# A new order of all operations in an attention-then-feed-forward kernel, with one store moved ahead of the next loads

## The chip, the cores and the metric

The kernel runs on one core of a Trainium2 chip. A core has five engines that run side by side, each through its own queue in order: TensorE (PE; its weight loads are listed as PEld), VectorE (DVE), ScalarE (ACT), GpSimd (POOL) and SyncE (SP). The last two, here, mainly issue DMAs. The metric is device microseconds of one execution, as a median over runs. A profile is one further execution with every instruction recorded.

## What is computed

Linear attention with cosine and sine weights, then a feed-forward block with a squared ReLU. There are 8 batches of 8 heads, 576 positions and 64 channels; the block works on 4608 tokens of 512 values with a hidden width of 2048.

```python
def phi(x, c, s):
    r = np.maximum(x, 0.0)
    return np.concatenate([r * c, r * s], axis=-1)
q_p = phi(q, cos_w, sin_w)
k_p = phi(k, cos_w, sin_w)
kv = np.einsum('bhsf,bhsd->bhfd', k_p, v)
z = np.sum(k_p, axis=2)
num = np.einsum('bhsf,bhfd->bhsd', q_p, kv)
den = np.einsum('bhsf,bhf->bhs', q_p, z)[..., None] + 1e-06
x = (num / den)  # heads beside each other: 4608 x 512
h = x @ w_in
r = np.maximum(h, 0.0)
g = r * r
out = g @ w_out
```

## The kernel before

Each batch goes through two parts. In the attention part, keys, queries and values are loaded (`ldk`, `ldq`, `ldv`: `load_main` at L513, `load_v` at L526), turned into features by eight wide operations (`cos` and `sin`, `feature` at L448), values are cast into a shared tile (`vs`, `spread_v` at L536), the matrix kv is summed on TensorE (`kv`, `mm_kv`) and copied out (`kvz`). Query features are transposed by DMA (`qTd`, L670), multiplied with kv (`num`), divided on VectorE (`div`: an add, a reciprocal and a product) and transposed by DMA again (`xTd`, L679). One load tile `kq` holds keys and queries of a batch, and from batch 2 on a feature operation handles both at once, so it needs both loads. The last 64 of the 576 positions are tails; two batches share a tile for them (`ldkt`, `ldqt`, and the operations with `t` or `.4` in their names).

In the feed-forward part both matrix products are done, from a point in batch 2 on, with seven block products in place of eight (Strassen-Winograd): `G{batch}.{quarter}.P1` to `P7` for the first (`plan_gemm1`, L960), `Y{batch}.P1` to `P7` for the second (`plan_pair`, L1159). `xs`, `S` and `w1s`, `w2t` are the sums of blocks that go in, made on VectorE. Results stand in PSUM banks and are taken out by ScalarE or VectorE: `seed`, `u2`, `s5` are copies, `c11r` and the like apply the ReLU and `c11q` the square. For `Y`, `c11`, `c12`, `c21`, `c22` write the four blocks of a batch's two output tiles `y`, and `st0` and `st1` store those two (512 KB each, `store` at L1089, issued by SP at L1097). There are two `y` tiles, so a batch's second tile is the one that the batch before stored with its `st1`: `Y2.c22` can only write when `Y1.st1` has landed. There are six PSUM banks for all products (`pool("x", 6)`) and one double bank for kv sums and numerators (`pool("n", 1)`): a product that needs a bank waits for the operation that empties it. For example `G3.3.P5` takes the bank that `Y2.c12` empties, and `num4.3` the one that `div4.1` empties.

What runs when is written out by hand, as a table of names: `ORDER` (L24 to L113). `Plan.run` (L220) takes it word by word; a `*` puts an operation on ScalarE that could be on either ScalarE or VectorE. The operations are issued in that order, so each engine's queue is the table's words for that engine, in the table's order. SP's queue holds loads, DMA transposes and stores, and a word there that must wait holds all that stand behind it. The same function assigns PSUM banks and tiles, from costs that stand beside each operation. A part before the table (`begin`, L1361) starts batch 0, and `loads_of_1` (L1490) issues batch 1's loads and weights on POOL's queue.

Four lines of the table before, round the place that matters:

```python
G3.0.P3 vs4.1* G3.0.c11r* G3.1.P1 Y2.P6 G3.0.u2* xs3.3 G3.0.P7 ldk5 div3.4 xs3.4 cos4.tk* kv4
ldv5.0 G3.1.seed G3.1.P2 ldq5 Y2.S3 Y2.u2* Y2.c11* Y1.st1 kvz4* G3.1.P6 num4.0 vs5.2 G3.0.c22r
...
G3.1.c21r* Y2.s5* G3.2.c11r* num4.1 div4.1 xTd3.2 vs5.0 sin5.3 G3.2.P6 G3.2.u2* Y2.P7 Y2.c22
sin5.0 ldv5.1 xTd4.0 Y2.P3 Y2.c12 Y2.st0 num4.3 div4.3 xTd4.1 cos5.1* cos5.3* G3.2.P5 G3.3.P1
```

Of the kernel before, what the change touches and what calls it, by code (L numbers as in the profile page):

```python
# [35 lines left out]
w2t3 xTc1.2 num1.3 vs2.0 ldv2.1 xT1.0 div1.3 Y0.c01* Y0.b12 Y0.b13 Y0.b14 ldkt2 Y0.b15 Y0.c11
ldqt2 xTc1.0* H1.3.00.0 Y0.c10 H1.3.00r* xT1.3 xTc1.3* cos2.1 sin2.0 cos2.2 cos2.0* sin2.1*
H1.2.00.0 H1.2.00r* sin2.2* cos2.3 sin2.3 Y0.st1 H1.0.01.0 H1.1.11.0 H1.1.11r* cos2.tk vs2.1*
H1.0.11.0 H1.0.11r* sin2.tk H1.1.00.0 H1.1.00r H1.3.00q H1.2.10.0 H1.1.11q* qTd2.0 H1.2.10r
qTd2.1 H1.2.01.0 ldk3 ldv3.0 H1.1.10.0 H1.1.10r* H1.3.10.0 kv2 kvz2* H1.0.10.0 num2.1 ldv3.2  # L40
H1.2.01r* ldq3 H1.0.00.0 w2t2 w2t4 H1.3.10r* H1.3.10q* div2.1 H1.1.01.0 H1.0.00r H1.1.01r num2.2
div2.2 H1.2.11.0 H1.0.01r* H1.1.01q H1.1.00q* H1.0.10r* H1.1.10q H1.3.11.0 H1.3.01.0 H1.2.11r*
H1.3.11r* H1.3.11q Y0.st0 num2.3 H1.3.01r* H1.3.01q Y1.P10 Y1.P11 div2.3 xTd2.1 Y1.seed Y1.P20
Y1.seed1 num2.0 vs3.0* Y1.S1 Y1.P21 vs3.2* Y1.P5 ldv3.1 Y1.S2 Y1.P6 ldv4.2 H2.1.10.0 cos3.1*
H2.0.11.0 div2.0 xTd2.0 sin3.1 cos3.0 sin3.0* qTd3.0 sin3.3* Y1.S3 Y1.u2 Y1.P7 cos3.3* H2.1.10r*
H2.0.11r* H2.0.00.0 Y1.c111* H2.1.00.0 sin3.2 cos3.2 qTd3.1 xs2.3 Y1.c110 xs2.1 xs2.2 vs3.1*
H2.0.00r ldq4 kv3 Y1.S4 xs2.4 H2.1.00r* vs4.2* G2.2.P1 kvz3 ldv4.0 sin3.tq H2.0.01.0 H2.0.01r
ldk4 num3.0 H2.1.11.0 div3.0 Y1.s5* Y1.c22 cos3.tq* G2.2.seed H2.1.11r* H2.1.11q H2.0.10.0
H2.1.00q* num3.1 div3.1 H2.0.10r* H2.1.01.0 w1s3 H2.1.01r* H2.1.01q* Y1.P3 H2.1.10q* num3.2
Y1.c12 div3.2 G2.2.P2 G2.2.c11r* vs4.0* G2.2.P6 ldkt4 G2.2.u2 G2.2.P5 G2.3.P1 G2.3.seed ldv5.2  # L50
ldkt5 num3.3 qTd3.2 xTd3.0 div3.3 G2.2.s5* G2.3.P5 G2.3.s5* G2.2.P7 G2.2.c22r G2.3.P2 G2.3.c11r*
G2.3.P6 xTd3.1 G2.3.u2 G2.2.P3 G2.2.P4 ldv4.1 cos4.1* G2.3.c11q G2.3.P3 sin4.1* Y1.st0 G2.3.P7
cos4.0 G2.3.c22r Y2.P1 cos4.3 sin4.0 G2.2.c21r* G2.2.c12r qTd4.0 cos4.2* G2.3.P4 G2.3.c21r
sin4.3* Y2.seed num3.4 Y1.P4 sin4.2 qTd4.1 G2.3.c21q* xs3.1 G3.0.P1 G3.0.P5 Y2.P2 G2.3.c12r
G2.3.c12q G2.3.c22q* G3.0.seed G3.0.P2 xs3.2 G3.0.P6 Y1.c21* Y2.S1 Y2.S2 sin4.tk G3.0.s5*
G3.0.P3 vs4.1* G3.0.c11r* G3.1.P1 Y2.P6 G3.0.u2* xs3.3 G3.0.P7 ldk5 div3.4 xs3.4 cos4.tk* kv4
ldv5.0 G3.1.seed G3.1.P2 ldq5 Y2.S3 Y2.u2* Y2.c11* Y1.st1 kvz4* G3.1.P6 num4.0 vs5.2 G3.0.c22r
G3.0.P4 ldqt1 G3.0.c12r div4.0 G3.1.c11r* G3.1.u2* G3.0.c21r* G3.1.P5 G3.1.s5* G3.1.P7 G3.1.c22r
G3.2.P1 G3.2.seed Y2.S4 num4.2 div4.2 G3.1.P3 Y2.P5 G3.1.c12r G3.1.P4 G3.2.P2 G3.1.c11q*
G3.1.c21r* Y2.s5* G3.2.c11r* num4.1 div4.1 xTd3.2 vs5.0 sin5.3 G3.2.P6 G3.2.u2* Y2.P7 Y2.c22  # L60
sin5.0 ldv5.1 xTd4.0 Y2.P3 Y2.c12 Y2.st0 num4.3 div4.3 xTd4.1 cos5.1* cos5.3* G3.2.P5 G3.3.P1
G3.3.P5 cos5.2 G3.2.s5* G3.2.P3 G3.2.P7 G3.2.c22r G3.2.c12r G3.3.seed G3.3.P2 G3.3.P6 G3.3.s5*
G3.3.P3 G3.2.P4 G3.3.u2* G3.3.c11r* sin5.2* G3.2.c21r* cos5.0 ldqt0 sin5.1 qTd5.0 G3.3.P7
G3.3.c22r Y2.P4 G3.3.c11q qTd5.1 G3.1.c21q* vs5.1* ldv6.2 ldv6.0 G3.3.P4 G3.3.c22q* Y3.P1
G3.3.c12r G3.3.c12q G3.3.c21r ldk6 Y3.seed xs4.1 G4.0.P1 G4.0.P5 G3.1.c12q* G4.0.seed G4.0.s5*
G3.3.c21q xs4.2 G3.1.c22q Y3.S1 Y3.S2 xs4.4 kv5 Y3.P2 kvz5* num5.0 Y3.S4 Y2.c21* G4.0.P6
G4.0.u2* xs4.3 sin1.tq* G4.0.P2 G4.0.c11r* G4.1.P1 G4.0.P3 div5.0 G4.0.c12r Y3.c11* Y3.P6 ldq6
G4.1.seed num5.2 div5.2 G4.0.P7 G4.0.c22r cos1.tq* Y3.u2* G4.1.P2 G4.1.c11r* G4.1.P6 G4.1.u2*
ldkt6 qTd1.2 vs6.0* Y2.st1 G4.1.P5 G4.2.P1 G4.0.P4 G4.0.c21r* Y3.S3 G4.1.P7 Y3.P5 ldkt7 G4.1.s5
G4.1.P3 G4.1.c22r G4.1.P4 G4.1.c22q ldv6.1 vs6.2 num5.3 G4.1.c12r G4.2.seed G4.1.c21r* G4.2.P6  # L70
G4.2.u2* div5.3 xTd5.1 G4.2.P2 G4.2.P5 G4.2.c11r* Y3.s5* G4.3.P1 G4.3.seed G4.2.s5 cos6.1*
num5.1 div5.1 xTd5.0 Y3.P7 sin6.3 sin6.1 num1.4 G4.2.P3 sin6.0 G4.2.c12r cos6.0* G4.3.P6
G4.3.u2* Y3.c22 G4.2.P7 div1.4 G4.3.P2 qTd6.0 G4.2.c22r xTd1.2 Y3.P3 cos6.3* G4.1.c21q*
G4.3.c11r* vs6.1 G4.3.P5 G4.3.s5* G4.3.c11q G4.3.P7 cos6.tk* sin6.tk* G4.2.P4 G4.3.c22r Y3.c12
G4.3.P3 sin6.2 Y3.P4 G5.0.P1 G4.3.P4 cos6.2* Y3.st0 kv6 G4.3.c12r G4.3.c22q G4.2.c21r* xs5.1
G5.0.P5 xs5.3 Y3.c21* qTd6.1 G5.0.seed G5.1.P1 G4.1.c12q ldv7.0 kvz6* G5.0.P2 num6.0 G4.3.c21r
xs5.2 xs5.4 G5.0.s5* G5.0.P3 ldq7 G5.1.seed G4.1.c11q* G5.0.P6 G5.0.u2* G4.3.c21q* G5.1.P2
div6.0 G5.0.c11r* Y4.P1 Y4.seed G4.3.c12q ldk7 Y4.S3 num6.1 div6.1 xTd6.0 G5.0.P7 G5.0.c22r
G5.0.c12r G5.1.c11r* G5.1.P6 Y4.P2 Y4.S1 G5.1.P5 G5.2.P1 Y4.S2 G5.1.u2* G5.1.P7 G5.1.s5* G5.1.P3
G5.1.c22r vs7.0* Y3.st1 ldqt5 num6.2 G5.0.P4 G5.0.c21r* Y4.c11* div6.2 Y4.P6 Y4.u2 G5.1.P4  # L80
G5.2.P5 ldv7.2 G5.1.c21r* Y4.S4 G5.2.s5* G5.2.seed G5.1.c12r num6.3 div6.3 G5.1.c12q* Y4.P5
G5.2.P6 G5.2.u2 G5.2.P2 G5.2.c11r G5.2.P3 cos7.3* G5.3.P1 G5.2.P7 Y4.P7 cos7.0* ldqt4 G5.3.seed
G5.2.c12r cos7.2 sin7.1* Y4.s5 G5.3.P6 G5.3.P2 ldv7.1 G5.3.P5 G5.3.u2* G5.3.P7 Y4.c22 cos7.1
# [12 lines left out]
Y5.c21* G7.0.P5 xs7.2 G7.0.P6 xs7.4 G6.3.c21r Y5.st0 G6.1.c21q* G6.2.c21r* G7.1.P1 G6.3.c21q
Y6.seed Y6.P2 G7.0.c11r xs7.3 G6.3.c12q Y5.st1 Y6.S1 G7.1.seed G7.1.P2 G7.0.u2* G7.0.s5* G7.0.P7
# [1518 lines left out]
```

## Time and profile before

| what | us |
|---|---|
| three runs, median (lowest to highest) | 273.77 (273.76 to 274.44) |
| the profiled execution | 273.22 |
| its span, first to last instruction | 271.2 |
| TensorE busy | 262.9 |
| VectorE busy | 225.5 |
| ScalarE busy | 186.1 |

Rows of the profile read as follows. In order of time: start and duration in microseconds, engine, source line, operation, tile written and tiles read, shapes, count, and in brackets how long the engine stood idle before it and what ended that. Groups by line: count, then busy time and mean nanoseconds of one, then idle time before them. DMA issues: tile and source, queue, count, size of each, and the median time from issue to landing; where the count is 1 that is the time of that one transfer. Stretches: from and to, length, then busy time and number of instructions for PE, PEld, DVE, ACT and POOL, the granted TensorE clock, the DMA share and GB/s. All matmuls stand on one line (L463), so they are told apart by the tiles: `ha`, `hb`, `hc` are the banks of the first product, `ya`, `yb`, `yc` those of the second.

### The profile page before, as it was taken

To read this page: it belongs to the slowest core of one execution; us is meant where nothing else is said; L and a number is where in the kernel's file an instruction comes from. 1 tells how busy PE (TensorE), PEld (TensorE's weight loads), DVE (VectorE), ACT (ScalarE), POOL (GpSimd) and SP (SyncE) were. 2 spreads that over 40 slices of the span, in tenths; PEclk is the share of its full clock that TensorE was granted. 3 is DMA by queue.
4 is the path that set the end of the run, shared out by engine and by line. 5 is a ranking of instruction groups with operands and counts; after the bars stand their busy time and mean duration, and the time that the engine had idled before them with its cause. 6 is when DMAs were issued, how large, how long until landed. Compare 5 with 4: busy or idle time off the path is not lost.

```text
span 271.2 us, 6727 instructions
## 1 busy us (share of the span) xinstructions
PE 262.9 (97%) x2775; PEld 224.2 (83%) x2780; DVE 225.5 (83%) x408; ACT 186.1 (69%) x288; POOL 24.9 (9%) x40
## 2 busy tenths in 40 slices
PE   8899999999999999989999999999999999999993
PEld 3578756799988889979998998898888888888882
DVE  3775995998999999799999999998979878877921
ACT  5755883688868998669879867995546466743610
POOL 8752241300000000000000000000000000000000
PEclk9999999999999999999999999999999999999999
DMA  6999999899999999999999999391623001010116
GB/s 219 232 206 269 304 200 325 164 258 338 278 210 350 197 201 282 327 221 212 330 240 218 207 369 255 42 258 34 176 39 156 22 2 79 33 47 0 80 39 196
DMA packets 84894, 51.62 MB, mean 190 GB/s; under 512 B 55808, under 2 KB 81408, under 8 KB 84864
## 3 DMA queue, kind: packets, MB, share of 16 engines
q1 hardware_dynamic: 73664, 38.94, 57.9%
q0 software_dynamic: 10608, 11.73, 20.7%
q10 hardware_dynamic: 592, 0.52, 0.7%
q8 instruction: 22, 0.36, 0.6%
q14 instruction: 8, 0.07, 0.1%
HBM read 36.70 MB, written 9.44 MB: 170 GB/s over the span
## 4 chain that ended last, share of the span: by engine, by line
PE 89%; DMA 5%; ACT 2%; DVE 2%; issue 1%; POOL 1%; POOLq 0%; DVEq 0%
PE ya L463 16%; PE yb L463 15%; PE hps L463 13%; PE hb L463 12%; PE hc L463 8%; PE ha L463 8%; PE yh L463 5%; PE num L463 4%; PE kz L463 3%; DMA xTt<-xpt 3%; PE yc L463 3%; DMA kq<-in_q_dram 2%; PE tq L653 1%; ACT gT L444 1%; PE tx L657 1%
## 5 line engine op out<-in xcount | busy, mean ns | idle before, releaser
L463 PEld LDWEIGHTS <-w1sb 128*128 128x128 bf16 x736 | 70.5, 98 | 9.3 <-DMA xT<-xp 0.3
L463 PEld LDWEIGHTS <-gs 128*128 128x128 bf16 x512 | 49.9, 98 | 5.7
L463 PEld LDWEIGHTS <-gT 128*128 128x128 bf16 x448 | 43.1, 98 | 9.6
L444 ACT ACTIVATE gT<-gT 128x1024 bf16<-128x1024 bf16 x35 | 36.4, 1054 | 2.1 <-DVE gT L457 1.5
L463 PE MATMUL hps<-xT,w1sb 128*128 128x256 bf16 x320 | 37.7, 273 | 0.0
L450 ACT ACTIVATE fe<-kq,cols 128x1024 bf16<-128x1024 f32 (+1 forms) x36 | 34.1, 989 | 3.1 <-DMA kq<-in_q_dram 1.5
L463 PEld LDWEIGHTS <-w1s 128*128 128x128 bf16 x312 | 29.7, 98 | 4.8 <-issue 1.4
L452 DVE TENSOR_SCALAR fe<-kq,cols 128x1024 bf16<-128x1024 f32 (+1 forms) x44 | 26.7, 642 | 4.7 <-DMA kq<-in_k_dram 3.2
L463 PE MATMUL ya<-w2sb,gT 128*128 128x256 bf16 x256 | 30.6, 273 | 0.0
L463 PE MATMUL hb<-xs,w1sb 128*128 128x256 bf16 x208 | 30.4, 272 | 0.1
L446 DVE TENSOR_TENSOR gT<-gT 128x1024 bf16<-128x1024 bf16 x37 | 25.1, 684 | 2.7 <-ACT gT L438 2.4
L463 PE MATMUL ha<-xT,w1sb 128*128 128x256 bf16 x176 | 26.1, 273 | 0.0
L438 ACT ACTIVATE gT<-hps 128x512 bf16<-128x512 f32 x28 | 16.2, 596 | 10.3 <-PE hps L463 10.3
L636 DVE TENSOR_TENSOR xp<-num,den 128x512 bf16<-128x512 f32 (+1 forms) x33 | 22.2, 675 | 1.1
L457 DVE CUSTOM_DVE_ANT_0 gT<-hb,s 128x512 bf16<-128x512 f32 x26 | 17.8, 685 | 5.3 <-PE hb L463 4.5
L434 ACT COPY hb<-ha 128x512 f32<-128x512 f32 x26 | 15.2, 586 | 8.1 <-DVE gT L457 2.5
L460 DVE TENSOR_TENSOR gs<-gT 128x2048 bf16<-128x2048 bf16 x16 | 19.5, 1218 | 0.5
L434 ACT COPY s<-hc 128x512 f32<-128x512 f32 x21 | 12.2, 586 | 10.2 <-PE hc L463 10.2
L457 DVE CUSTOM_DVE_ANT_0 gT<-hc,u 128x512 bf16<-128x512 f32 x26 | 17.7, 682 | 1.8 <-ACT u L434 1.5
L438 ACT ACTIVATE gT<-ha 128x512 bf16<-128x512 f32 x22 | 13.1, 597 | 6.4 <-PE ha L463 6.4
L463 PE MATMUL hc<-xs,w1s 128*128 128x256 bf16 x104 | 15.6, 273 | 1.3 <-DVE y L460 1.3
L463 PE MATMUL hb<-xs,w1s 128*128 128x256 bf16 x104 | 15.4, 273 | 0.0
(113 smaller groups left out, 406.1 us busy)
## 6 DMA issues: line engine op xcount, KB each, us to landing
out_dram<-y SPq DMA_DIRECT2D x16, 512.0 KB, 3.7
kq<-in_k_dram SPq DMA_DIRECT2D x5, 1024.0 KB, 8.1
vs<-in_v_dram SPq DMA_DIRECT2D x10, 512.0 KB, 6.4
kq<-in_q_dram SPq DMA_DIRECT2D x5, 1024.0 KB, 9.5
w1sb<-in_moe_w_in_dram POOLq DMA_DIRECT2D x4, 512.0 KB, 10.8
w2sb<-in_moe_w_out_dram POOLq DMA_DIRECT2D x4, 512.0 KB, 12.6
kq<-in_q_dram POOLq DMA_DIRECT2D x2, 1024.0 KB, 10.6
kq<-in_k_dram POOLq DMA_DIRECT2D x2, 1024.0 KB, 13.0
```

The costliest lines, as they stand in the source:

```text
L434: (nc.scalar.copy if e == "ACT" else nc.vector.tensor_copy)(out=out, in_=in_)
L438: nc.scalar.activation(out=out, in_=in_, func=ACTF.Relu)
L444: nc.scalar.activation(out=out, in_=in_, func=ACTF.Square)
L446: nc.vector.tensor_tensor(out=out, in0=in_, in1=in_, op=ALU.mult)
L450: nc.scalar.activation(out=out, in_=in_, func=ACTF.Relu, scale=col)
L452: nc.vector.tensor_scalar(out=out, in0=in_, scalar1=0.0, scalar2=col, op0=ALU.max, op1=ALU.mult)
L457: nc.vector._custom_dve(dve_ops.TENSOR_ADD_SAT, out=out, in0=in0, in1=in1, s0=BIG, s1=0.0)
L460: nc.vector.tensor_tensor(out=out, in0=in0, in1=in1, op=op)
L463: nc.tensor.matmul(out=out, lhsT=lhsT, rhs=rhs, start=start, stop=stop, skip_group_check=True)
L636: nc.vector.tensor_tensor(out=x, in0=n4[:, :, :, 0:D].rearrange("p b (k l) d -> p b k l d", l=2), in1=r.rearrange("p b (k l) -> p b k l", l=2)
L653: nc.tensor.transpose(t[:, h, :], fe[b, j // 2][:, 1, j % 2, h, :], ident[:, :])
L657: nc.tensor.transpose(t[:, kb, :], xp[b, j // 2][:, kb, j % 2, :], ident[:, :])
```

## The change

Only the table changes: the same operations with the same dependencies, in another order, and 33 of them on the other of the two engines (22 from VectorE to ScalarE, 11 from ScalarE to VectorE). TensorE has the same 374 operations, many neighbours of them exchanged. On SP's queue `Y1.st1` now stands ahead of `ldk5`, `ldv5.0` and `ldq5`; `Y2.st1` stands ahead of `ldk6`, which has changed places with `ldq6`; `ldqt0` is issued earlier, behind `ldqt1`; and some tail loads, transposes and stores have changed places with a neighbour. On POOL's queue `ldqt2` and `ldkt2` come ahead of `ldv2.1`. The words of the places that the prediction speaks of, cut from the diff:

```diff
...
-G3.0.P3 vs4.1* G3.0.c11r* G3.1.P1 Y2.P6 G3.0.u2* xs3.3 G3.0.P7 ldk5 div3.4 xs3.4 cos4.tk* kv4
-ldv5.0 G3.1.seed G3.1.P2 ldq5 Y2.S3 Y2.u2* Y2.c11* Y1.st1 kvz4* G3.1.P6 num4.0 vs5.2 G3.0.c22r
-G3.0.P4 ldqt1 G3.0.c12r div4.0 G3.1.c11r* G3.1.u2* G3.0.c21r* G3.1.P5 G3.1.s5* G3.1.P7 G3.1.c22r
-G3.2.P1 G3.2.seed Y2.S4 num4.2 div4.2 G3.1.P3 Y2.P5 G3.1.c12r G3.1.P4 G3.2.P2 G3.1.c11q*
-G3.1.c21r* Y2.s5* G3.2.c11r* num4.1 div4.1 xTd3.2 vs5.0 sin5.3 G3.2.P6 G3.2.u2* Y2.P7 Y2.c22
-sin5.0 ldv5.1 xTd4.0 Y2.P3 Y2.c12 Y2.st0 num4.3 div4.3 xTd4.1 cos5.1* cos5.3* G3.2.P5 G3.3.P1
...
+G2.3.c12r G2.3.c12q G2.3.c22q* G3.0.seed G3.0.P2 Y1.c21* Y1.st1 ldk5 xs3.2 Y2.S1 G3.0.P6 Y2.S2
...
+div3.4 cos4.tk* kv4 ldv5.0 vs5.2* G3.0.c22r G3.1.seed ldq5 Y2.S3 G3.1.P2 Y2.u2* kvz4* G3.1.P6
+num4.0 G3.0.P4 ldqt1 ldqt0 div4.0 G3.1.c11r* G3.1.u2* G3.0.c12r G3.0.c21r* G3.1.P5 G3.1.P7
+G3.1.s5* G3.1.c22r G3.2.P1 G3.2.seed num4.2 Y2.S4 div4.2 G3.1.P3 vs5.0 xTd3.2 Y2.P5 Y2.s5*
+G3.1.c12r G3.1.P4 G3.2.P6 G3.1.c21r* G3.1.c11q G3.2.P2 G3.2.c11r* num4.1 div4.1 G3.2.u2* sin5.3
+ldv5.1 Y2.P7 Y2.c22 sin5.0 xTd4.0 Y2.P3 Y2.c12 Y2.st0 num4.3 G3.2.P5 G3.3.P1 div4.3 xTd4.1
...
-ldkt6 qTd1.2 vs6.0* Y2.st1 G4.1.P5 G4.2.P1 G4.0.P4 G4.0.c21r* Y3.S3 G4.1.P7 Y3.P5 ldkt7 G4.1.s5
...
+Y3.S4 Y2.c21* Y2.st1 G4.0.P6 G4.0.P2 G4.0.c11r* G4.1.P1 G4.0.P3 G4.0.u2* Y3.c11* G4.0.c12r Y3.P6
...
-G7.3.c11r* G7.3.c11q* G7.3.P6 G7.3.u2 G7.3.s5 Y6.P3 G7.3.P7 G7.3.P3 G8.0.P1 Y6.c12 G8.0.seed
-G7.2.P4 G7.3.c22r G7.3.c22q* G7.3.P4 G7.3.c21r* Y6.P7 Y6.st0 G8.0.P2 G8.0.c11r* G7.3.c12r xs8.1
...
+G7.1.c22q G7.2.P7 Y6.S3 G7.2.c22r G7.3.P2 G7.3.c11r* G7.3.u2 Y6.P3 G7.3.P7 G7.3.c22r G7.3.c11q*
+G8.0.P1 Y6.u2* Y6.c12 Y6.st0 G7.2.P4 G7.3.P3 G7.3.c12r G7.3.P4 G7.3.c22q* G7.3.c21r* Y6.P7
...
```

The table after ends with the same copies and stores as before, in nearly the same order.

## Prediction

> **What bounds the kernel now.** I read a table of busy time by stretch first, then the instructions in order of time round the one long wait of TensorE, then the DMA queue there.
>
> ```profile
> 0.00:20.00 20.00, 17.69 (x171) 10.38 (x173) 11.92 (x35) 12.05 (x21) 14.36 (x27) 1.00 1.08 219
> 20.00:100.00 80.00, 79.78 (x857) 65.84 (x860) 70.24 (x129) 62.03 (x93) 10.56 (x14) 1.00 1.14 261
> 100.00:120.00 20.00, 18.73 (x224) 16.84 (x223) 17.14 (x35) 14.15 (x23) 0.00 (x0) 1.00 1.04 283
> 120.00:220.00 100.00, 100.00 (x1105) 89.72 (x1104) 91.47 (x164) 73.97 (x116) 0.00 (x0) 1.00 0.74 175
> 220.00:266.70 46.70, 46.64 (x426) 41.42 (x424) 34.30 (x49) 23.87 (x37) 0.00 (x0) 1.00 0.15 54
> 266.70:271.20 4.50, 0.01 (x1) 0.00 (x0) 0.42 (x1) 0.00 (x0) 0.00 (x0) 0.95 0.52 158
> ```
>
> TensorE (the second figure of each stretch, after its length) is the bound, and its granted clock (third from last) is 1.00 while it works. Its idle time is 2.31 us in the first 20 us, 0.22 up to 100, 1.27 from 100 to 120, nothing up to 220, 0.06 up to the last matmul, and 4.49 us of tail. An order can only add or remove such gaps. One is long:
>
> ```profile
> 115.41 0.60 PE L463 MATMUL hc<-xs,w1s 128*128 128x256 bf16 x4
> 115.85 0.60 PE L463 MATMUL ha<-xT,w1sb 128*128 128x256 bf16 x4
> 117.72 0.60 PE L463 MATMUL hc<-xs,w1s 128*128 128x256 bf16 x4 [1.27 <-DVE y L460]
> ```
>
> Groups of four matmuls start 0.44 us apart (115.41, 115.85). So G3.3.P5, which began at 117.72, could have begun at 116.29: 1.43 us lost. Its PSUM bank is freed by Y2.c12 on VectorE (DVE). What made that late:
>
> ```profile
> 109.43 0.16 DVE L630 TENSOR_SCALAR den<-num 128x8 f32<-128x8 f32 x1
> ...
> 109.86 0.69 DVE L636 TENSOR_TENSOR xp<-num,den 128x512 bf16<-128x512 f32 x1
> 110.47 0.68 DVE L457 CUSTOM_DVE_ANT_0 gT<-hc,u 128x512 bf16<-128x512 f32 x1
> ...
> 112.49 0.68 DVE L434 CAST vext<-vs 128x1024 bf16<-128x1024 f32 x1
> 114.07 0.75 DVE L452 TENSOR_SCALAR fe<-kq,cols 128x1024 bf16<-128x1024 f32 x1 [0.90 <-DMA kq<-in_q_dram]
> 115.72 0.69 DVE L460 TENSOR_TENSOR y<-yb,ys 128x512 f32<-128x512 f32 x1 [0.90 <-DMA out_dram<-y]
> 116.33 0.74 DVE L452 TENSOR_SCALAR fe<-kq,cols 128x1024 bf16<-128x1024 f32 x1
> 116.99 0.68 DVE L460 TENSOR_TENSOR y<-ya,yu 128x512 f32<-128x512 f32 x1
> ```
>
> In the kernel's names these are div4.2 (109.43 to 110.47), G3.1.c12r, vs5.0, sin5.3, Y2.c22, sin5.0, Y2.c12. There are two waits in a row of 0.90 us: sin5.3 for batch 5's query load ldq5, then Y2.c22 for batch 1's second store, Y1.st1, whose y buffer it writes. SP's queue and the time to landing (last column) say why:
>
> ```profile
> 103.20 0.57 SPq L514 DMA_DIRECT2D kq<-in_k_dram  x1
> 103.89 0.57 SPq L529 DMA_DIRECT2D vs<-in_v_dram  x1
> 104.51 0.51 SPq L514 DMA_DIRECT2D kq<-in_q_dram  x1
> 105.06 2.32 SPq L1097 DMA_DIRECT2D out_dram<-y  x1
> 107.48 0.63 SPq L522 DMA_DIRECT2D kqt<-in_q_dram  x1
> ```
> ```profile
> kq<-in_k_dram SPq DMA_DIRECT2D x1, 1024.0 KB, 5.6
> kq<-in_q_dram SPq DMA_DIRECT2D x1, 1024.0 KB, 9.5
> vs<-in_v_dram SPq DMA_DIRECT2D x1, 512.0 KB, 7.5
> out_dram<-y SPq DMA_DIRECT2D x1, 512.0 KB, 10.5
> kqt<-in_q_dram SPq DMA_DIRECT2D x1, 128.0 KB, 8.3
> ```
>
> Start plus time to landing: ldk5 108.8, ldv5.0 111.4, ldq5 114.0, Y1.st1 115.6, ldqt1 115.8. They land in the order of issue, 2.6, 2.6, 1.6 and 0.2 us apart, though 103.89 and 105.06, for example, are only 1.2 us apart at issue: each waits for the one in front. The store is late only because it stands behind 2.5 MB of loads.
>
> **The change, part by part.** (1) *The store in front.* Y1.st1 now stands ahead of ldk5, ldv5.0 and ldq5. Its input, Y1.c21, is ready by then:
>
> ```profile
> 98.59 0.58 ACT L434 COPY y<-yb 128x512 f32<-128x512 f32 x1
> ```
>
> That ends at 99.2, four us before the slot at 103.20, so the store holds nothing up at issue, and it lands ahead of ldk5. Y2.c22's wait of 0.90 us disappears. But the same four transfers still need the same time: by the queue's order all three loads land one store later. What a store in front costs has no row of its own; from below it is 0 (it overlaps the loads), from above 1.6 us plus a pause when the queue turns from writing to reading, and for that pause there are two rows. Behind Y1.st1 the next load landed 0.2 us later. Behind Y2.st1:
>
> ```profile
> 137.74 0.58 SPq L1097 DMA_DIRECT2D out_dram<-y  x1
> 138.37 0.63 SPq L522 DMA_DIRECT2D kqt<-in_k_dram  x1
> ```
> ```profile
> out_dram<-y SPq DMA_DIRECT2D x1, 512.0 KB, 4.0
> kqt<-in_k_dram SPq DMA_DIRECT2D x1, 128.0 KB, 4.7
> ```
>
> 141.7 and 143.1: 1.4 us for an equal 128 KB. So the price lies in 0 to 1.6 + 1.2 = 2.8 us; I take 1.6, since every landing above follows its predecessor. ldv5.0 then lands at 113.0 and ldq5 at 115.6.
>
> The Trainium skill, "DMA: Bandwidth & Descriptors", section "Two DMAs through the same engine are not ordered", says that descriptors of a queue start in order but are pipelined, and that an engine's read and write sides are separate queues. By that rule the store's writes could run beside the loads' reads and cost them nothing; the rows above show neither this order nor a saving. By the rule the total would be that of rival A, by the rows that of the forecast.
>
> (2) *VectorE's order at the same place.* The new table has, after div4.2: vs5.0, G3.1.c12r, G3.1.c11q (a square, moved here from ScalarE), div4.1, sin5.3, Y2.c22, sin5.0, Y2.c12. Before, c12r and div4.1 came first. So now vs5.0, which waits for ldv5.0, holds all of them. Start-to-start steps: 0.61 for a 512-column operation (109.86 to 110.47, also 115.72 to 116.33), 1.04 for a division (109.43 to 110.47), 0.66 for a feature (116.33 to 116.99), 0.73 from Y2.c12's start to TensorE (116.99 to 117.72). I give vs5.0 (0.68 long like c12r) and the square the step of 0.61 too:
>
> ```profile
> L446 DVE TENSOR_TENSOR gT<-gT 128x1024 bf16<-128x1024 bf16 x37 | 25.1, 684 | 2.7 <-ACT gT L438 2.4
> ```
>
> 113.0 + 3 x 0.61 = 114.83 div4.1; + 1.04 = 115.87 sin5.3 (ldq5 is there at 115.6, so it no longer decides); + 0.66 + 0.61 + 0.66 + 0.73 = 118.53 for G3.3.P5, where it was 117.72: **0.81 us later**, not 1.43 earlier. Part of it shows sooner on TensorE: num4.3 needs the bank that div4.1 frees at 115.87; it stood at 115.17 before. ScalarE has cos5.1 and cos5.3 behind ldq5, and G3.2.s5 behind them:
>
> ```profile
> 114.07 2.19 ACT L450 ACTIVATE fe<-kq,cols 128x1024 bf16<-128x1024 f32 x2 [1.25 <-DMA kq<-in_q_dram]
> ```
>
> From 115.6 the two features end at 117.8; the copy (0.58 us, like the one at 98.59) at 118.4; its reader G3.2.P3 comes two groups of matmuls after 118.53, at 119.4: covered by 1.0 us.
>
> (3) *A small stall goes.* Before, G7.3.c22r stood behind Y6.c12 on VectorE:
>
> ```profile
> 225.04 0.69 DVE L460 TENSOR_TENSOR y<-ya,yu 128x512 f32<-128x512 f32 x1 [0.72 <-ACT gT L444]
> 225.65 0.68 DVE L457 CUSTOM_DVE_ANT_0 gT<-hb,s 128x512 bf16<-128x512 f32 x1
> ```
> ```profile
> 226.38 0.31 PEld L463 LDWEIGHTS <-w1sb 128*128 128x128 bf16 x3 [0.23 <-issue]
> ```
>
> VectorE idled before 225.04, and c22r's end (226.33) released the weights at 226.38. Now c22r precedes c12: -0.2 us.
>
> (4) *Everything else.* 33 operations change engine (22 to ScalarE, 11 to VectorE), none leaves or joins TensorE. VectorE loses 11 x 0.68 = 7.5 us; the bound engine feels none of it, since it idled 0.06 us from 120 to 266.7. Without that cover, one late operation costs its own 0.6 to 0.7 us. Y2.st1 also moves, ahead of batch 6's key load, which becomes the last of that batch at 139.0 + 1.6 = 140.6:
>
> ```profile
> 128.44 0.95 SPq L514 DMA_DIRECT2D kq<-in_q_dram  x1
> ```
> ```profile
> kq<-in_q_dram SPq DMA_DIRECT2D x1, 1024.0 KB, 10.6
> ```
> ```profile
> 141.52 2.20 ACT L450 ACTIVATE fe<-kq,cols 128x1024 bf16<-128x1024 f32 x2
> ```
>
> The first feature starts at 141.5: 0.9 us of cover is left. ldqt0 puts its 0.63 us of issue (as ldqt1 at 107.48) ahead of xTd3.2, which only the batch of tails reads, at the end. The swaps among small loads, transposes and the last stores, and POOL's two tail loads ahead of ldv2.1, fall where TensorE idles 0.22 us in 80 or less; the tail still ends with the same copies and stores. I price them at 0, between -0.3 and +0.5.
>
> Sum: 0.81 - 0.2 = **+0.6 us**. The profiled execution took 273.22 us (271.2 of span, 2.0 around it), the three runs 273.76 to 274.44 with median 273.77. On the median: **274.4 us**, 0.2% up. I call 0.3% (0.8 us) the least that can be told from no change.
>
> **The rivals.** *A: the store costs the loads nothing* (not slower). The landings stay at 111.4 and 114.0; the chain of part 2 from 111.4 gives 116.93, which is 0.79 less than 117.72; with part 3, 1.0 us less: 272.8. Were the loads to come earlier still, the floor is 1.43 + 0.2: 272.1. For it: writes and reads go opposite ways. Against: the landings one behind the other. *B: turning from writing to reading costs extra* at this place. From the first tenth on it passes straight to TensorE, as vs5.0 has no slack left: with 1.2 us, 275.6. For it: the 1.4 us behind Y2.st1; against: the 0.2 behind Y1.st1. *C: the order does not reach the time*: ldv5.0 lands by 112.7, ldq5 at 115.6 decides, 115.6 + 2.66 = 118.26 is 0.54 later, part 3 takes 0.2 off, and the new order of the first 20 us, whose gaps sum to 2.31 us, takes off the other 0.3: 273.8. Nothing in the rows points to that gain.
>
> **How the numbers follow.** Forecast 0.45, A 0.25, B 0.22, C 0.08. The forecast's own range is 273.9 to 275.2, split evenly by 274.6: 0.22 slower, 0.23 same. A gives 0.21 faster and 0.04 same, B 0.22 slower, C 0.06 same and 0.01 on each side. Faster 0.22, same 0.33, slower 0.45. The range takes in most of A and B: 272.4 to 276.2.
>
> **What would show it.** Right: Y1.st1 lands within 5 us of issue, no VectorE wait for a store near 115, a new VectorE wait of about 2 us for batch 5's values (vs) near 110 to 113, and TensorE waiting near 115 to 118 for num or hc. Wrong: ldv5.0 landing by 111.5 after its old issue time (then A), or after 114 (then B), or a TensorE wait of half a us anywhere else.

## The result, and the profile after

| kernel | median of its runs, us (lowest to highest) | ratio to before, 95% interval |
|---|---|---|
| before, 12 runs beside the change | 273.87 (272.73 to 275.32) | |
| changed, 12 runs | 276.06 (274.44 to 280.34) | 1.0072 (1.0048 to 1.0097) |
| changed, once more (e1), 6 runs | 277.73 (274.73 to 279.32) | 1.0145 (1.0096 to 1.0194) |

The change makes the kernel slower, by more than the 0.6 us that were forecast: 1.3 to 2.7 us by the first interval, more by the second. A ratio compares runs taken beside each other and leaves disturbed executions out, so it can differ from the quotient of the two medians (for e2 below by 0.7%). The profile kept of the changed kernel is that of its longest run, 280.34 us; e1's profile is of its shortest, 274.73 us, and the text says where the two differ.

First the busy time by stretch, before and after (length, then busy time of PE, PEld, DVE, ACT and POOL, granted TensorE clock, DMA share, GB/s):

```profile
20.00:110.00 90.00, 89.78 (x989) 74.96 (x992) 79.61 (x148) 70.40 (x106) 10.56 (x14) 1.00 1.13 262
110.00:130.00 20.00, 18.73 (x219) 16.81 (x218) 17.55 (x31) 14.77 (x23) 0.00 (x0) 1.00 1.04 243
```
```profile
20.00:110.00 90.00, 88.00 (x965) 73.09 (x967) 73.08 (x137) 74.48 (x112) 10.71 (x15) 1.00 1.10 250
110.00:130.00 20.00, 16.84 (x145) 13.59 (x144) 13.74 (x26) 10.78 (x17) 0.00 (x0) 0.83 1.06 249
130.00:220.00 90.00, 90.00 (x1013) 80.72 (x1011) 79.31 (x145) 68.31 (x107) 0.00 (x0) 1.00 0.79 183
```

Three things went wrong, and the prediction spoke of one. TensorE idles 2.00 us from 20 to 110 (0.22 before). It idles 3.16 us from 110 to 130 (1.27 before). And in that stretch its mean clock was 0.83. The list of TensorE's waits in the changed kernel (us in total, times, longest) names the places:

```profile
PE num L464 <- DVE xp L637: 1.7, 1, 1.7
PE hc L464 <- DVE y L461: 1.5, 1, 1.5
...
PE hps L464 <- DMA w1sb<-in_moe_w_in_dram: 0.9, 2, 0.7
PE num L464 <- DMA qpTt<-fet: 0.5, 1, 0.5
PE hps L464 <- DMA xT<-xp: 0.5, 1, 0.5
```

The figures count from the modelled end of the group before. Where the text below speaks of time lost, it counts from when the next group could have begun, 0.44 us after the start of the one before, which is 0.17 us more for each wait. The first two are num4.3 and G3.3.P5, where the forecast put the loss. The other three are waits for transfers, at 20.9, 97.0 and 79.3 us; the first profile of before has none of this size there. e1 has two of them again:

```profile
PE hc L464 <- DVE y L461: 1.3, 1, 1.3
...
PE num L464 <- DVE xp L637: 0.7, 1, 0.7
PE hps L464 <- DMA xT<-xp: 0.7, 1, 0.7
PE hps L464 <- DMA w1sb<-in_moe_w_in_dram: 0.5, 1, 0.5
```

Now the place of the store: SP's queue (start, time to issue) and the time from issue to landing (last column) in the changed kernel.

```profile
106.35 0.52 SPq L1098 DMA_DIRECT2D out_dram<-y  x1
106.92 0.42 SPq L515 DMA_DIRECT2D kq<-in_k_dram  x1
107.46 1.24 SPq L530 DMA_DIRECT2D vs<-in_v_dram  x1
108.75 0.74 SPq L515 DMA_DIRECT2D kq<-in_q_dram  x1
```
```profile
kq<-in_k_dram SPq DMA_DIRECT2D x1, 1024.0 KB, 8.3
kq<-in_q_dram SPq DMA_DIRECT2D x1, 1024.0 KB, 11.0
out_dram<-y SPq DMA_DIRECT2D x1, 512.0 KB, 4.9
vs<-in_v_dram SPq DMA_DIRECT2D x1, 512.0 KB, 9.2
```

The store lands at 111.2, then ldk5 at 115.2, ldv5.0 at 116.7, ldq5 at 119.7. To compare executions in which everything is shifted, I count from the landing of batch 4's last query transposes, which are issued just ahead (105.63 before, 108.56 after, by the trace). ldq5 landed 8.4 us behind them before, 11.2 after, 10.7 in e1: 2.3 to 2.7 us later, where 1.6 were forecast. VectorE in order:

```profile
116.71 0.69 DVE L435 CAST vext<-vs 128x1024 bf16<-128x1024 f32 x1 [3.39 <-DMA vs<-in_v_dram]
117.32 0.68 DVE L458 CUSTOM_DVE_ANT_0 gT<-hc,u 128x512 bf16<-128x512 f32 x1
117.92 0.68 DVE L447 TENSOR_TENSOR gT<-gT 128x1024 bf16<-128x1024 bf16 x1
118.52 0.16 DVE L631 TENSOR_SCALAR den<-num 128x8 f32<-128x8 f32 x1
...
119.79 0.76 DVE L453 TENSOR_SCALAR fe<-kq,cols 128x1024 bf16<-128x1024 f32 x1 [0.15 <-DMA kq<-in_q_dram]
120.46 0.68 DVE L461 TENSOR_TENSOR y<-yb,ys 128x512 f32<-128x512 f32 x1
```

The wait for the store in front of Y2.c22 (120.46) is gone, as it should be. But vs5.0 (116.71) waits 3.39 us for its load, and the chain that the forecast wrote down follows: c12r, c11q, div4.1 (118.52), sin5.3, Y2.c22. On TensorE:

```profile
119.69 0.42 PE L464 MATMUL num<-kvz,qpT 128*128 128x65 bf16 x8 [1.69 <-DVE xp L637]
...
122.45 1.01 PE L464 MATMUL hc<-xs,w1s 128*128 128x256 bf16 x4 [1.47 <-DVE y L461]
```

The last row shows one more thing: four matmuls took 1.01 us there; such a group takes 0.60 elsewhere. That is the clock, which was granted at 0.50 there (last section).

### The profile page after: what moved, and what is told of

Read it like the earlier page. It is cut to its first block, busy times and chain, and to the rows that moved or that the text cites. A ratio compares the mean times of both kernels' runs of the same rounds, so it can differ in the third digit from the quotient of the medians.

```text
span 278.3 us, 6718 instructions
## 1 busy us (share of the span) xinstructions
PE 266.6 (96%) x2775; PEld 225.9 (81%) x2780; DVE 219.2 (79%) x397; ACT 193.8 (70%) x299; POOL 24.4 (9%) x40
## 4 chain that ended last, share of the span: by engine, by line
PE 79%; DMA 12%; DVE 3%; POOL 3%; issue 1%; ACT 0%; SPq 0%; DVEq 0%; POOLq 0%
PE ya L464 14%; PE yb L464 13%; PE hps L464 11%; PE hb L464 11%; PE hc L464 8%; PE ha L464 8%; PE yh L464 5%; DMA w1sb<-in_moe_w_in_dram 4%; DMA kq<-in_q_dram 4%; PE kz L464 3%; PE num L464 3%; DMA xT<-xp 2%; PE yc L464 2%; DMA qpTt<-fet 1%; POOL kq L515 1%
## 5 line engine op out<-in xcount | busy, mean ns | idle before, releaser
L464 PEld LDWEIGHTS <-w1sb 128*128 128x128 bf16 x736 | 71.3, 99 | 11.4 <-DMA w1sb<-in_moe_w_in_dram 1.3
L445 ACT ACTIVATE gT<-gT 128x1024 bf16<-128x1024 bf16 x40 | 41.9, 1058 | 8.7 <-DVE gT L458 4.9
L451 ACT ACTIVATE fe<-kq,cols 128x1024 bf16<-128x1024 f32 (+1 forms) x35 | 33.0, 985 | 6.4 <-DMA kq<-in_k_dram 2.9
L464 PEld LDWEIGHTS <-w1s 128*128 128x128 bf16 x312 | 30.4, 100 | 5.8 <-issue 1.6
L464 PE MATMUL hb<-xs,w1sb 128*128 128x256 bf16 x208 | 31.2, 278 | 0.0
L453 DVE TENSOR_SCALAR fe<-kq,cols 128x1024 bf16<-128x1024 f32 (+1 forms) x45 | 27.9, 663 | 3.6 <-DMA kq<-in_k_dram 3.5
L464 PE MATMUL ha<-xT,w1sb 128*128 128x256 bf16 x176 | 26.7, 276 | 0.0
L447 DVE TENSOR_TENSOR gT<-gT 128x1024 bf16<-128x1024 bf16 x32 | 21.6, 684 | 0.2
L439 ACT ACTIVATE gT<-hps 128x512 bf16<-128x512 f32 x31 | 17.5, 596 | 5.0 <-PE hps L464 4.9
```

Of the source, the lines that this page charges most:

```text
L439: nc.scalar.activation(out=out, in_=in_, func=ACTF.Relu)
L445: nc.scalar.activation(out=out, in_=in_, func=ACTF.Square)
L447: nc.vector.tensor_tensor(out=out, in0=in_, in1=in_, op=ALU.mult)
L451: nc.scalar.activation(out=out, in_=in_, func=ACTF.Relu, scale=col)
L453: nc.vector.tensor_scalar(out=out, in0=in_, scalar1=0.0, scalar2=col, op0=ALU.max, op1=ALU.mult)
L464: nc.tensor.matmul(out=out, lhsT=lhsT, rhs=rhs, start=start, stop=stop, skip_group_check=True)
```

## The experiments

Two theories at the start. *The store*: its turn at the queue is passed on to the loads, VectorE works in order and passes the delay to TensorE; all of the loss comes from that one word. *The rest of the order*: the loss lies in the waits at 20.9, 79.3 and 97.0 us, or elsewhere. Times below are medians, with the ratio to the kernel before and its interval.

**e1: the changed kernel again, no edit.**

> The changed kernel once more, for a profile at full TensorE clock beside the first one, and for the time. Theory 1 (the store's time is passed on to the three loads behind it, and vs5.0 and ldq5 then hold VectorE): ldv5.0 lands 7.4 to 8.5 us and ldq5 10 to 11.5 us after the transpose qTd4.1 (5.8 and 8.4 before the change), num4.3 and G3.3.P5 together lose 2.3 to 3.5 us (1.4 before), the time is 1 to 2.5 us above the kernel before. Theory 2 (the loss lies in the rest of the new order or in the TensorE clock): those two lose 1.5 us or less in this profile and the time is still 2 us up, with gaps of 0.5 us or more elsewhere or a granted clock under 0.99.

277.73 us, ratio 1.0145 (1.0096 to 1.0194). In the profile (274.73 us) ldq5 landed 10.7 us behind the transposes, num4.3 and G3.3.P5 waited, and so did TensorE at 20.0 and 78.7. So the two waits that the forecast named are no matter of one execution. The wait at 97.0 was absent here, and the clock stayed full. The waits near 20 and 79 us are less clearly the new order's: single ones of 0.6 to 0.8 us turn up in later profiles in which this part of the order is the old one (at 20.7 in e4 and e7, at 78.3 in e11).

**e2: the changed kernel, vs5.0 put back behind div4.1.**

```diff
 G3.1.P3
-vs5.0
 xTd3.2
...
 div4.1
+vs5.0
 G3.2.u2*
```

> The new order with one word moved: vs5.0 behind div4.1 on VectorE, as it was before the change. Theory 1: num4.3 no longer waits, G3.3.P5 waits for ldq5 alone (landing + 2.7 us); since ldq5 lands 1 to 1.3 us later than what vs5.0's chain needs, nearly all of the loss stays: 0.1 to 0.6 us less than e1_after_again. A theory in which vs5.0's place is the cause: 1 us or more less than e1_after_again.

278.61 us, ratio 1.0109 (1.0067 to 1.0150): not to be told from e1 by these intervals. num4.3 no longer waits, but G3.3.P5 waits 3.19 us in one piece, since sin5.3 stands there for ldq5 (10.8 us behind the transposes). The place of vs5.0 only chooses which product shows the delay first.

**e3: the kernel before, the store alone moved.**

```diff
 G3.0.P7
+Y1.st1
 ldk5
...
 Y2.c11*
-Y1.st1
 kvz4*
```

> The kernel before with one word moved: Y1.st1 in front of ldk5, everything else in the old order. Theory 1: ldq5 lands 1.6 to 2.7 us later than before, Y2.c22 no longer waits for the store, G3.3.P5 begins at ldq5 + 2.7 us: 0.5 to 1.7 us slower than the kernel before. Theory 2 and rival A of the prediction (the store costs the loads nothing): ldq5 at its old distance from qTd4.1, G3.3.P5 1 us earlier, the time 0.8 to 1.0 us below the kernel before.

275.19 us, ratio 1.0060 (1.0030 to 1.0089). SP's queue, and the times to landing:

```profile
104.95 0.52 SPq L1097 DMA_DIRECT2D out_dram<-y  x1
105.53 0.42 SPq L514 DMA_DIRECT2D kq<-in_k_dram  x1
106.06 1.28 SPq L529 DMA_DIRECT2D vs<-in_v_dram  x1
107.40 0.94 SPq L514 DMA_DIRECT2D kq<-in_q_dram  x1
```
```profile
kq<-in_k_dram SPq DMA_DIRECT2D x1, 1024.0 KB, 7.3
kq<-in_q_dram SPq DMA_DIRECT2D x1, 1024.0 KB, 10.1
out_dram<-y SPq DMA_DIRECT2D x1, 512.0 KB, 5.1
vs<-in_v_dram SPq DMA_DIRECT2D x1, 512.0 KB, 8.2
```

Landings 110.0, 112.8, 114.3, 117.5; ldq5 10.7 us behind the transposes (106.76), 2.3 more than before. All four together end 0.7 us later than before (10.7 against 10.0 behind the transposes; 11.2 in the changed kernel): the store's own turn of 1.6 us plus 0.7 to 1.2. The trace shows where the extra goes. In the first 4 us behind the transposes the DMA engines moved 363 GB/s before, with a load in front, and 268 here, with the store in front (last figure; 266 to 299 in the changed kernel, e1 and e2):

```profile
105.63:109.63 4.00, 4.00 (x51) 3.63 (x49) 3.57 (x9) 3.57 (x6) 0.00 (x0) 1.00 1.06 363
```
```profile
106.76:110.76 4.00, 4.00 (x45) 3.62 (x43) 3.56 (x7) 2.77 (x5) 0.00 (x0) 1.00 0.97 268
```

What is missing there would take about 1.0 us at the rate before (an estimate from these two rows). Whether it is a pause between writing and reading or a slower store no run separates. VectorE and TensorE follow:

```profile
114.26 0.69 DVE L434 CAST vext<-vs 128x1024 bf16<-128x1024 f32 x1 [1.36 <-DMA vs<-in_v_dram]
117.55 0.75 DVE L452 TENSOR_SCALAR fe<-kq,cols 128x1024 bf16<-128x1024 f32 x1 [2.59 <-DMA kq<-in_q_dram]
```
```profile
120.21 0.78 PE L463 MATMUL hc<-xs,w1s 128*128 128x256 bf16 x4 [3.43 <-DVE y L460]
```

Nothing else in this kernel waits: TensorE's busy time from 20 to 110 us is 89.79, as before. The profile is of the longest of its runs (277.44 us), so the wait of 3.43 us need not be typical. One word moved, with nothing else changed, costs about 1.6 us by the ratio, at the place that the forecast named and from store to loads to VectorE to TensorE, though here, with vs5.0 in its old place, sin5.3 and ldq5 are the links that decide.

**e4: the kernel before, Y2.c22 (which waits for the store) behind Y2.c12.** The other way to get rid of the wait, without moving a transfer.

```diff
 Y2.P7
-Y2.c22
 sin5.0
...
 Y2.c12
+Y2.c22
 Y2.st0
```

> The kernel before with the store where it was, and Y2.c22 (which waits for it) moved behind Y2.c12 on VectorE, so that it holds nothing that TensorE needs soon. Theory 1: G3.3.P5 begins at ldq5's landing + 2.0 us, 116.1 to 116.6 in place of 117.7; a gap of 0.2 to 0.7 us may come back at G3.2.P3 or G3.2.P4. The time is 0.7 to 1.3 us below the kernel before. If the wait for the store was not what held TensorE there, no change.

A miss: 274.44 us, ratio 1.0015 (0.9988 to 1.0042). G3.3.P5's wait is gone, and nothing came of it. In this profile TensorE lost 1.41 us at G3.0.P5, at 100.2 us, waiting for sums of a late transpose, 0.56 us at 20.7 and 0.34 at 104.5, all of it ahead of the word that was moved. That asks how fixed the waits of the kernel before are (e8).

**e5: the changed kernel, the store alone put back.**

```diff
 Y1.c21*
-Y1.st1
 ldk5
...
 ldq5
+Y1.st1
 Y2.S3
```

> The changed kernel with one word of its order moved: batch 1's second store goes back behind batch 5's query load. All else of the new order stays, vs5.0 ahead of div4.1 too. First theory (the store's turn at the queues is passed on to the loads, and VectorE, which runs in order, passes it on to TensorE): ldv5.0 lands again 5.8 us after the transposes and ldq5 8.4 us after them, as in the kernel before; the waits of num4.3 and G3.3.P5 together fall under 1.5 us, the TensorE clock stays granted in full round 120 us, and the time is 273.2 to 274.2 us. Rival (the loss lies in the rest of the new order: the waits for transposes at H0.2.00.0, H2.0.00.0 and num3.4): these stay at 0.6 to 0.9 us each, and the time stays at 275.5 us or more.

275.42 us, ratio 1.0034 (1.0004 to 1.0064). ldv5.0 and ldq5 land 6.0 and 8.5 us behind the transposes, as before, and the clock is full. G3.3.P5 waits 1.66 us, near the 1.43 of the first profile of before. But the waits at 20.4 (0.73), 79.6 (0.87) and 97.3 us (0.61) stay, with others at 60.0 (0.55) and 108.1 (0.80). Here the store theory fell as an explanation of the whole: without the store's move some of the loss is still there.

**e6: the store in front, and the evacuations ahead of vs5.0 and the features.**

```diff
 G3.0.P7
+Y1.st1
 ldk5
...
 Y2.c12
+vs5.0
+ldv5.1
+sin5.3
+sin5.0
 Y2.st0
```

(vs5.0, ldv5.1, sin5.3 and sin5.0 leave their places ahead of Y2.c12; cos5.1 and cos5.3 go behind G3.3.seed and G3.3.u2.)

> The kernel before with the store in front of the three loads of batch 5, and on VectorE the two evacuations Y2.c22 and Y2.c12 ahead of vs5.0, sin5.3 and sin5.0 (ldv5.1, cos5.1 and cos5.3 a little later with them). First theory: ldq5 lands 10.5 to 11 us after the transposes, as late as with the store alone, but nobody frees a bank behind it: the wait of G3.3.P5 (3.60 us with the store alone) falls under 0.7 us, about 1.1 us come back at G3.2.P4, where its turn on VectorE is now later, no stretch of half clock, time 273.6 to 274.6 us. Rival (late loads cost the end by themselves, through the features of batch 5, whatever VectorE's order): the time stays at the 275.2 us of the store alone.

A miss: 275.54 us, ratio 1.0053 (1.0027 to 1.0079). G3.3.P5 no longer waits, but ldq5 landed 12.2 us behind the transposes, and the features now stand ahead of the next evacuations:

```profile
119.61 0.60 PE L463 MATMUL hc<-xT,w1s 128*128 128x256 bf16 x4 [0.79 <-ACT s L434]
121.72 1.03 PE L463 MATMUL hb<-xs,w1sb 128*128 128x256 bf16 x8 [1.51 <-DVE gT L457]
```

The delay of a load is not removed by reordering its first reader; it waits at the next thing behind that reader.

**e7: the kernel before, three features ahead of Y2.c12, no DMA moved.**

```diff
 sin5.0
+cos5.2
+cos5.0
+sin5.1
 ldv5.1
...
 G3.3.P5
-cos5.2
...
 G3.2.c21r*
-cos5.0
 ldqt0
-sin5.1
```

> The kernel before, the store where it was, no load moved; on VectorE three feature operations of batch 5 (cos5.2, cos5.0, sin5.1), 0.61 us each by their rows, go in front of the evacuation Y2.c12. That makes the one long wait of TensorE longer by VectorE's order alone: 1.43 + 3 x 0.61 = 3.3 us at G3.3.P5. First theory with the clock (a wait of about 3 us is followed by a stretch at half the TensorE clock, whatever caused the wait): a stretch of 3.4 or 6.8 us at half clock begins within 3.5 us of the wait's end and adds 1.6 to 3 us; the time is 276.5 to 278.5 us. Rival (the half clock comes from the late transfers, or from chance): full clock throughout, time 273.8 + 1.8 = 275.6 us or less.

275.00 us, ratio 1.0029 (1.0002 to 1.0056), full clock. The long wait that was to be made didn't arise (0.80 us near 121): TensorE had already lost 2.3 us at 20.7, 99.8 and 104.0 in this execution, so VectorE was less behind. It says nothing of the clock.

**e8: the kernel before again, no edit.**

> The kernel before, once more, for how much its own waits differ between executions. If its waits are a matter of its order, G3.3.P5 waits 1.3 to 1.6 us again, no other wait of TensorE after 20 us is over 0.5 us, and ldq5 lands 8.2 to 8.6 us after the transposes. If they are a matter of the execution, waits of 0.5 us or more for transposes appear, as at H2.0.00.0 and G3.0.P5 in the runs of its altered copies.

273.09 us, span 271.0 as in the first profile (271.2). The wait at G3.3.P5, around which the prediction was built, is not there. In its place stand

```profile
98.51 0.61 PE L463 MATMUL hc<-xs,w1s 128*128 128x256 bf16 x4 [0.34 <-DVE xs L460]
102.79 1.92 PE L463 MATMUL yb<-w2t,gs 128*128 128x256 bf16 x16 [0.18 <-DVE gs L460]
```

and some lost time in the start. ldq5 landed at 113.90, against 114.04 in the first profile, but TensorE reached num4.3 at 116.52 in place of 115.17. Read together, the wait goes by when the transfers land; TensorE spends it at G3.3.P5 or earlier, and the time is the same. That would explain e4. The other profiles with the old early order fit it. In before, e3 and e6 the transpose xTd3.1 lands at 95.0 to 95.9, and TensorE does not wait near 100 us; in e4, e7, e8, e10, e11 and e12 it lands at 97.8 to 99.6, and TensorE loses 0.5 to 1.6 us at G3.0.P5, between 98 and 101 us and ahead of every edit. Why one order gives both is open.

**e9: the new order up to the store's slot (376 words), then the old one, the store where it was.** The diff is against the new table.

```diff
 Y1.c21*
-Y1.st1 ldk5 xs3.2 Y2.S1 G3.0.P6 Y2.S2
...
+xs3.2 G3.0.P6 Y2.S1 Y2.S2 sin4.tk G3.0.s5*
...
```

> The new order for everything that stands in it ahead of batch 1's second store (376 operations, up to about 97 us), then the old order for the rest, the store where the old order has it. Theory now: the new order loses in two places, in its early part (the waits of TensorE at H2.0.00.0 and num3.4, 0.6 to 0.9 us each in the changed kernel, that the kernel before doesn't have) and by the store in front of the loads. Then this kernel keeps the early waits (H2.0.00.0 and the one near 97 us, together 0.9 to 1.5 us) and has the loads as in the kernel before (ldq5 8.2 to 8.6 us after the transposes), full clock, time 274.6 to 275.6 us. Rival (the early waits are paid back later, since the stretch round 100 to 120 us waits for transfers anyway, as the second execution of the kernel before had its waits near 100 us instead of at G3.3.P5): 273.5 to 274.1 us.

275.85 us, ratio 1.0069 (1.0041 to 1.0097): as slow as the whole change by its first measurement, with the store and all words of the late part as before; the idea that early waits are paid back later falls. Two things that were expected did not come: no wait at H2.0.00.0, and ldq5 landed 10.0 us behind the transposes, not 8.4. Two early waits on TensorE (the kernel sums of batch 2, and num3.4), and the longest one:

```profile
59.78 1.09 PE L463 MATMUL kz<-vext,fe 128*128 128x65 bf16 x31 [0.45 <-ACT vext L434]
...
96.37 0.60 PE L463 MATMUL num<-kvz,qpTt 128*64 128x65 bf16 x16 [0.40 <-DMA qpTt<-fet]
...
120.74 0.60 PE L463 MATMUL hc<-xT,w1s 128*128 128x256 bf16 x4 [2.28 <-ACT s L434]
```

The longest is not shown to come from the early order. TensorE waits there for a copy on ScalarE that stands behind two features, and these wait for ldq5. By the trace ldq5's landing is told in 16 steps: 15 had come by 116.18, 8.2 us behind the transposes, and the last came at 118.01. Nor is this profile, of the longest run of e9 (276.88 us), typical. So the price of the early part is taken from the 12 runs; of its 1.9 us the profile places about one, as TensorE idles 1.27 us from 20 to 110, against 0.22 and, in e8, 0.51 before.

The wait at num3.4 is legible in the queue. SP before, then in e9:

```profile
87.14 3.59 SPq L670 DMA_TRANSPOSE qpTt<-fet  x1
90.83 2.60 SPq L679 DMA_TRANSPOSE xT<-xp  x2
```
```profile
88.60 4.61 SPq L679 DMA_TRANSPOSE xT<-xp  x1
93.27 1.30 SPq L670 DMA_TRANSPOSE qpTt<-fet  x1
```

qTd3.2, the transpose that num3.4 reads, now stands behind xTd3.0, whose issue is held until 93.2. By the trace it lands at 96.33, 92.78 before; 1.1 us of that is xTd3.0's turn (it lands at 95.25), the rest a later queue. The wait of the kernel sums goes back to a load of batch 2's values, ldv2.1, which POOL now issues behind two loads of tails: it landed at 58.66, 54.55 before, and the copy on ScalarE that reads it, which didn't wait before, waits 2.04 us:

```profile
58.69 1.05 ACT L434 COPY vext<-vs 128x1024 bf16<-128x1024 bf16 x1 [2.04 <-DMA vs<-in_v_dram]
```

ldv2.1 lands at 57.9 to 58.9 in all five profiles with the new early order and at 54.5 to 56.4 in the nine with the old one, and waits of TensorE near 60 and 97 us appear in the new order's profiles alone (three and four of the five). Which of the exchanges in the early part costs how much was not tried one by one.

**e10: the old order up to ldk5 (390 words), then the new one, the store behind ldq5.** The diff is against the old table.

```diff
 G3.0.P7
-ldk5 div3.4 xs3.4 cos4.tk* kv4
+ldk5 xs3.4 Y2.c11* div3.4 cos4.tk* kv4 ldv5.0 vs5.2* G3.0.c22r G3.1.seed ldq5 Y1.st1
...
```

> The old order up to batch 5's key load (390 operations, up to about 102 us), then the new order for the rest, but with the store behind ldq5 as in the old order. Theory: the late part of the new order costs nothing beside the store; no wait at H2.0.00.0 over 0.4 us, ldv5.0 5 to 6 us and ldq5 8.2 to 8.6 us behind the transposes, waits from 110 to 125 us under 1.6 us in all; time 273.4 to 274.2 us. Rival (vs5.0 ahead of div4.1 and the new order behind it lose by themselves): num4.3 and G3.3.P5 wait 2 us or more together, time 274.8 us or more.

273.22 us, ratio 0.9979 (0.9957 to 1.0001): no slower than before, perhaps 0.6 us faster, which the interval does not quite settle. From 110 to 130 us TensorE doesn't idle; but neither does it in the second execution of the kernel before (e8, the second row), so the row by itself is no gain:

```profile
110.00:130.00 20.00, 20.00 (x231) 18.11 (x230) 19.39 (x37) 15.30 (x23) 0.00 (x0) 1.00 1.06 245
```
```profile
110.00:130.00 20.00, 20.00 (x232) 18.12 (x230) 18.97 (x34) 15.58 (x24) 0.00 (x0) 1.00 1.02 240
```

It has the lowest median of the altered kernels: the late half of the new order, without the word that the change is named for.

**e11: the store in front and the three features of e7** (the two diffs together).

> The kernel before with the store in front of the three loads and, besides, three feature operations of batch 5 (cos5.2, cos5.0, sin5.1; 0.61 us each) in front of the evacuation Y2.c12 on VectorE: the wait of G3.3.P5, 3.60 us with the store alone, grows to about 3.6 + 1.8 = 5.4 us in the same place. If a long wait of TensorE brings the half clock, a wait of 5 us brings it in nearly every execution, where 3 us did it in some (2 of 12 with the store alone): mean clock at or under 0.994 in 10 or more of 12 runs, a stretch of 3.4 or 6.8 us at half clock begins before or within 3.5 us of the wait's end, time 277.5 to 280 us. Rival (the half clock comes by chance, whatever TensorE waits): clock under 0.995 in at most 3 of 12 runs, and the time is 275.2 + 1.8 = 277.0 us or less.

276.60 us, ratio 1.0109 (1.0063 to 1.0154), 6 runs. A miss for what it was to show: the wait came in two pieces, 1.23 us at 120.1 and 1.74 at 122.7, the profile has full clock, and 2 of the 6 runs had a mean clock under 0.995.

**e12: the kernel before with ldq5 ahead of the store and ldv5.0.**

```diff
 kv4
-ldv5.0
 G3.1.seed
...
 ldq5
+Y1.st1
+ldv5.0
 Y2.S3
...
 Y2.c12
+vs5.0
+ldv5.1
 Y2.st0
```

> A candidate. The kernel before with batch 5's loads in the order ldk5, ldq5, store, ldv5.0, so that the query load, which VectorE's features wait for, comes a load of 2.6 us earlier; vs5.0 and ldv5.1 move behind the evacuation Y2.c12. Theory (what stands in front of VectorE's evacuations sets TensorE's wait): ldq5 lands 5.5 to 6.3 us after the transposes, G3.3.P5 doesn't wait, nothing over 0.6 us from 105 to 120 us, and ldv5.0, now last, lands 11 us or more after the transposes; a wait of up to 1.4 us may come at G4.0.P1, which needs the last transposes of batch 4. Time 272.6 to 273.8 us. Rival (the stretch is bound by the transfers as a whole, so a wait that goes in one place comes back in the next): 273.8 to 275 us.

274.87 us, ratio 1.0030 (1.0002 to 1.0057). ldq5 lands 7.4 us behind the transposes (a us earlier, not 2.6), G3.3.P5 doesn't wait, and 1.55 us are lost at G3.0.P5 (99.3) and 0.58 at G4.0.P5 (127.0). As in e4, the wait is gone and nothing is gained; as it is gone in e8 too, the profile doesn't show that the edit removed it.

## Why the prediction came out as it did

The direction and the chain held, at one of two places: the changed kernel is slower, its store passes its time on to the loads, vs5.0 holds VectorE, num4.3 and then G3.3.P5 show it. The size was about a third of what the first measurement gave and less of the second, for two reasons. That 276.06 us lies inside 272.4 to 276.2 is in part luck: that range was drawn wide to take in rivals A and B, the forecast's own ended at 275.2, e1's 277.73 us lies outside both, and a good part of the loss came from exchanges that had been priced at nothing.

- **Part 1, the store: a term too small.** It was priced at 1.6 us of delay for ldv5.0 and ldq5, out of bounds of 0 and 2.8. In the changed kernel, e1, e2 and e3 ldq5 comes 2.3 to 2.7 us later (3.2 in e11, 3.8 in e6): the store's turn of 1.6 plus, in the first four of these, 0.7 to 1.2 us. That is rival B's size and place, and its 275.6 us is close to the 275.19 of the store alone; that the extra is a pause for turning from writing to reading, as B has it, is argued and not shown. Rival A is excluded by the landings. By the rule of the Trainium skill that it was set beside ("DMA: Bandwidth & Descriptors", "Two DMAs through the same engine are not ordered": read and write sides are separate queues) the store could have run beside the loads; no run here shows it doing so.
- **Part 2, VectorE's order: right as seen, but it prices nothing by itself.** vs5.0's wait, forecast as about 2 us, was 3.39 (2.36 in e1). "ldq5 no longer decides" was a near tie: sin5.3 still waited 0.15 us for it. With vs5.0 put back (e2) the time is no better, because ldq5 then decides alone.
- **Part 3: right.** The profile after has no wait of TensorE over 0.2 us behind 123 us.
- **Part 4, everything else at nothing: the step that failed.** The early part alone costs 0.41 to 0.97% (e9), no less than the store by these intervals. The argument was that its exchanges "fall where TensorE idles 0.22 us in 80 or less". That TensorE idles little says that nothing is late there now; it doesn't say how late a transfer may become. qTd3.2 had 2.0 us to spare (landing 92.78, num3.4 at 94.79), and the exchange with xTd3.0, with a later queue, took 3.6. The prediction did name "a TensorE wait of half a us anywhere else" as the sign that it was wrong, and the changed kernel has three such waits in its first profile and two in e1, though only the one at 97 us has no like in profiles with the old early order.
- **Left out: the clock.** "An order can only add or remove such gaps" has no term for it. The stretch at half clock in the changed kernel's first profile has 5.75 us of TensorE work, so about 2.9 us more without any gap (an estimate from its row in the last section). e1's profile has no such stretch, and its two named waits are there all the same.
- **The single long gap.** The 1.43 us at G3.3.P5 were read as what the change could win. e8 shows the same kernel and the same time without that wait, and e4 and e12, which were to take it away, gain nothing.

Do the parts add up? Early part +0.69%, late part -0.21%, together without the store +0.34% (e5); the store alone +0.60%; sum 0.94 to 1.08%, between the two measurements of the whole (0.72 and 1.45%). So the lost time has two sources, the early part and the store; which is the larger these intervals, each about 0.3% to either side, don't tell.

## What to carry to other kernels

The store put in front of the loads on one queue delayed the last of them by 2.3 to 2.7 us, more than the 1.6 us that it took behind them, so move a store ahead only where the loads' first readers have that much slack. For each transfer that an order shifts, compare its landing with its reader's start; an idle-free TensorE is no evidence of slack. When a whole order is replaced, splice old and new at a point where both can be cut: two such runs found here what a reading of the one named word missed, and a second profile of the old kernel tells which of its waits are fixed.

## What the hardware showed beside that

After the longest waits TensorE's clock was granted at half for a while. Stretches of the changed kernel and of e3 (clock third from last):

```profile
110.00:121.40 11.40, 9.29 (x101) 8.01 (x100) 7.72 (x15) 4.79 (x8) 0.00 (x0) 1.00 1.10 282
121.40:128.20 6.80, 5.75 (x28) 3.96 (x28) 4.64 (x9) 4.19 (x8) 0.00 (x0) 0.50 0.94 191
```
```profile
120.50:123.90 3.40, 3.40 (x18) 2.42 (x17) 2.42 (x4) 0.77 (x2) 0.00 (x0) 0.50 1.10 195
```

e2 has one too, from 123.0 to 126.4. Those of e3 and e2 last 3.4 us and begin 0.3 and 1.0 us behind waits of 3.60 and 3.19 us; the one of the changed kernel lasts 6.8 us and begins inside the second of two waits, 1.86 and 1.63 us, that end at 119.7 and 122.5. The other profiles have none, with 0.83 + 1.43 (e1), 1.23 + 1.74 (e11) or 2.44 + 0.67 + 0.34 (e9) in as short a time. The price shows in the runs: with the store alone, two of 12 had a mean clock of 0.991 and 0.993 and took 277.4 us, the other ten 274.5 to 275.5 at 0.995 or more. The Trainium skill, "TensorE: Matmul & The Clock Gate", Part 1, describes a free-running window of about 3.4 us and half clock after an idle one. The lengths agree with one and two windows; that a whole window must be idle does not, as no wait in the changed kernel lasted 1.9 us. From which idle share on it happens is open: e7 and e11 were to make one long wait and didn't. Runs of the kernel before with a mean clock near 0.99 also exist (nine of 87 in the three comparisons, 276.0 to 277.4 us), so it isn't the change's alone, and two of 12 are no more than that. But six of the 18 runs of the changed kernel and seven of the 12 of e2 lie under 0.995, and none of the 72 of e4, e5, e6, e7, e10 and e12, so it goes with the kernels that have the longest waits and makes these dearer than they look.
